# Attention and two feed-forward layers on one core: the first two blocks as one written list of single operations

## The chip, the cores and the metric

The kernel runs on one core of a Trainium2 chip. A core has TensorE (matmul, with its weight loads), VectorE, ScalarE, GpSimd and SyncE; in the profile they are PE (and PEld), DVE, ACT, POOL and SP. Each engine works through its own instructions in a fixed order and waits on semaphores for the others; data comes from and goes to device memory by DMAs, which SP, ACT and POOL issue. The metric is the device time of one execution in microseconds; of several executions the median counts.

## What is computed

Linear attention over 8 batches of 8 heads (576 positions, 64 wide) gives 4608 tokens of width 512. They go through a feed-forward layer with squared ReLU and then through one with SiLU, both 512 to 2048 to 512.

```python
def _attn_ref(q, k, v):
    q_s = np.exp(q - np.max(q, axis=-1, keepdims=True))
    q_s = q_s / (np.sum(q_s, axis=-1, keepdims=True) + 1e-09)
    k_s = np.exp(k - np.max(k, axis=2, keepdims=True))
    k_s = k_s / (np.sum(k_s, axis=2, keepdims=True) + 1e-09)
    kv = np.einsum('bhsd,bhse->bhde', k_s, v)
    return np.einsum('bhsd,bhde->bhse', q_s, kv)
def _moe_ref(x, w_in, w_out):        # then _moe2_ref, with h * sigmoid(h)
    r = np.maximum(x @ w_in, 0.0)
    return (r * r) @ w_out
# x = attention, tokens as rows: (4608, 512); out = _moe2_ref(_moe_ref(x))
```

The arrays are float32. For the layers the weights arrive as 64-bit words, of which the kernel makes a rounded float32 itself.

## The kernel before

The tokens are cut into 9 blocks of 512 (`NB`): block `i` below 8 holds the first 512 positions of batch `i`, block 8 the last 64 of every batch. A block has four pairs of heads (`pr` 0 to 3). For each pair the steps are: load keys, queries and values (`kv_load`, `q_load`, `v_load`; the remaining 64 positions of a batch come with `r_load`); the keys' maximum over positions (`kv_max`: three VectorE operations, then a transpose, a reduction, a scaled identity and a matmul that spreads it, `kv_tr`, `kv_red`, `kv_diag`, `kv_bc`; three pairs of block 0 use a GpSimd reduction over partitions instead); `kv_sub`, `kv_exp`, the product with the values `kv_mm`, the reciprocal `kv_rc` and the scaling `kv_scale`. Queries go through `q_max`, `q_sub`, `q_exp`, `q_norm`, `q_tr`, `q_hi`. Then `x_mm` gives the attention's output in PSUM, and `x_hi` (ScalarE) and `x_lo` (VectorE) split it into a high and a low float32r part.

The first layer has 16 column groups, here called weights 0 to 15. Each is loaded raw (`w1_load`), rounded (`w1_bits`, one ScalarE operation on the low words; `w1_round`, three VectorE operations: `TENSOR_SCALAR`, `SCALAR_TENSOR_TENSOR` and the custom integer addition) and split into a high part (`w1_hi`, ScalarE) and a low part (`w1_lo`, VectorE). For a block, a weight and a pair, `layer_part` issues three layer matmuls (high by high, high by low, low by high) into a bank `h`; four pairs make a group. `hidden` applies ReLU and square on ScalarE, `g_first` and `g_second` form sums for the next layer's Strassen-like products, `g_store` writes them to memory.

Every engine's instructions stay in the order in which the program writes them (`InOrder`, L73). For block 0, and for the attention of block 1, this order is a list of step names, `PLAN`; block 1's layer and all further blocks go through a loop over `n = i * 16 + t`, with steps hung into slots by the table `side` (`at`, `ORDER`, `SOONER`). After block 8 come three stages of Strassen-like products for the other three weight matrices; they take the time from about 500 us to the end.

SBUF is handed out as 73 rooms of one [128, 512] float32 each (`NU`; `room`, `back`, first in, first out). Raw weights of the first layer lie in three double rooms of `g_pool` and, early on, in the third of the `g_tiles`; rounded ones take a room (`wu`). The loop also rounds the second weight matrix to memory from block 3 on, through the same three double rooms. When block 8 starts, the rooms of the attention are given back, and the weights of the next stage are begun as rooms come free (`todo`, `begin`). The memory of `g_pool` becomes 9 further rooms after block 8.

Of the kernel before, what the change touches and what calls it, by code (L numbers as in the profile page):

```python
# [2 lines left out]

# [22 lines left out]
def kernel(  # L26
# [56 lines left out]
    P = 128  # L83
# [21 lines left out]
    PE_TR = (0, 1)  # L105

# [7 lines left out]
    NU = 73  # L114
# [3 lines left out]
    doubles, views = deque((-1, -2, -3, 0, 1, 2)), [0] * 3  # L118
    g_pool_was = tc.tile_pool(name="gpool", bufs=1)
    g_pool = g_pool_was.__enter__()  # L120

    def room(dt=F32, name="u"):
        n = rooms.popleft()
# [10 lines left out]
    def back(*ts):  # L134
        for t in ts:
            _, n, whence = lent.pop(id(t))
            whence.append(n)
# [28 lines left out]
    def raw_load(ph, f):  # L166

        if ph < 2:
            n = doubles.popleft()
            if n < 0:  # L170
                t = g_tiles[2].rearrange("p s c -> p (s c)").bitcast(I32)[:, 2 * TB * ~n:2 * TB * -n]
                lent[id(t)] = (t, n, doubles if views else [])
                views[:1] = []
            else:
                t = g_pool.tile([P, 2 * TB], I32, tag=f"d{n}", name="wraw")
                lent[id(t)] = (t, n, doubles)
            if ph:
                src = w_out[ph].bitcast(I32)[f * P:(f + 1) * P, :]
            else:
                src = w_in[ph].bitcast(I32)[:, 2 * f * P:2 * (f + 1) * P].rearrange(  # L180
                    "(c p) f -> p c f", p=P
                )
            sp.dma_start(out=t if ph else t.rearrange("p (c f) -> p c f", c=KC), in_=src)
            return [t]
# [50 lines left out]
    wh1, wl1, raw1 = {}, {}, {}  # L235

    def w1_load(x):
        raw1[x] = raw_load(*x)

    def w1_bits(x):  # L240
        to = []
        raw1[x] = to, rounding(0, raw1[x], to)
        next(raw1[x][1])

    def w1_round(x):
        to, going = raw1[x]
        for _ in going:
            pass
        raw1[x] = to[0]

    def w1_hi(x):
        wh1[x] = room(F32R, "wh")
        ac.copy(wh1[x], raw1[x])

    def w1_lo(x):
        u = raw1.pop(x)
        wl1[x] = room(F32R, "wl")
        ve.tensor_tensor(wl1[x], u, f32(wh1[x]), op=ALU.subtract)
        back(u)
# [112 lines left out]
    def kvf_store(b, pr):  # L372
        if pr == KC - 1:
            sp.dma_start(out=kvfd[b], in_=kvf_rooms[b % 2])
# [14 lines left out]
    kt, krt, vt, vrt, mt, mbt, held = {}, {}, {}, {}, {}, {}, {}  # L389

    def r_load(b, pr, dma=sp, dma2=sp):
# [3 lines left out]
        held[b] = [room(F32, "kr"), room(F32, "vr")]  # L395
        kr, vr = held[b][0], held[b][1][:, 0:KC * (D + 1)]
# [19 lines left out]
    def kv_load(b, pr, dma=sp):  # L416
# [15 lines left out]
        if b > 0 and pr == 0:  # L432
            r_load(b, pr)
# [27 lines left out]
    def kv_max(b, pr):  # L461
# [8 lines left out]
    mkt, kvps = {}, {}  # L470

    VIA_POOL = ((0, 1), (0, 2), (0, 3))
# [25 lines left out]
    def kv_sub(b, pr):  # L498
# [4 lines left out]
        )  # L503
        ve.tensor_tensor(tr, tr, mb, op=ALU.subtract)

    def kv_exp(b, pr):
        t, tr = kt[b, pr], krt[b, pr]
        ac.activation(t, t, AF.Exp)
        ac.activation(tr, tr, AF.Exp)


    def kv_mm(b, pr):
# [10 lines left out]
        if pr == KC - 1:  # L523
            back(*held.pop(b))
# [3 lines left out]
    def kv_rc(b, pr):  # L528
        rc = rct[b, pr] = spool.tile([P, 1], F32, tag="rc", name="rc", bufs=3)
        ve.tensor_scalar(rc, kvps[b, pr][:, 2 * P + D:2 * P + D + 1], EPS, None, op0=ALU.add)  # L530
        ve.reciprocal(rc, rc)
# [76 lines left out]
    def q_norm(i, pr):  # L608
# [3 lines left out]
        else:  # L612
            sm = spool.tile([P, 2, R, 1], F32, tag="sm", name="sm", bufs=6)
            ve.tensor_reduce(sm, t, axis=AX.X, op=ALU.add)
        ve.tensor_scalar(sm, sm, EPS, None, op0=ALU.add)
        ve.reciprocal(sm, sm)
        if i in PE_TR:
# [101 lines left out]
    def layer_part(t, c):  # L719
        if c == 0:  # L720
            first_h[t] = bank("h")
        h, f, (xh, xl) = first_h[t], FS[t], xs1[0, c]
# [4 lines left out]
        if t == NF - 1:  # L727
            back(*xs1.pop((0, c)))
# [3 lines left out]
    g_tiles.append(g_pool.tile([P, 7, TB], F32, tag="gs", name="gs"))  # L732

# [12 lines left out]
    def hidden(i, f, h):  # L746
# [6 lines left out]
        )  # L753
        ac.activation(o, o, AF.Square)
        back(h)

    def g_first(i, j):
        t = g_place(i, j)
        ve.tensor_tensor(t[:, S1], t[:, A21], t[:, A22], op=ALU.add)
        ve.tensor_tensor(t[:, S3], t[:, A11], t[:, A21], op=ALU.subtract)  # L760
# [17 lines left out]

    side = {}

    def at(i, slot, fn, *a):
        i, slot = divmod(max(0, i * NF + slot), NF)
        side.setdefault((i, slot), []).append((fn, a))
# [24 lines left out]
    at(1, 0, kvf_store, 1, KC - 1)  # L808
# [5 lines left out]
    for fn, d in ORDER:  # L814
        for nxt in range(2, NB):
            for pr, s in enumerate(BEGIN.get(nxt, (-12, -8, -4, 0))):
                if fn not in OF_KV or nxt < B:
                    if (fn, nxt, pr) in ((kv_load, 2, 0), (kv_load, 2, 1), (q_load, 2, 0)):
                        continue
# [285 lines left out]
    def store(u, half, ends):  # L1105
# [33 lines left out]
    wlist = [(0, f) for f in FS]  # L1139
    w2list = [(1, f) for f in range(NF)]  # L1140
    code_w = dict(w=w1_load, wbits=w1_bits, wround=w1_round, whi=w1_hi, wlo=w1_lo)
    code = dict(
        k=kv_load, q=q_load, v=v_load, kmax=kv_max, kred=kv_red, ksub=kv_sub, kexp=kv_exp,
        qmax=q_max, qsub=q_sub, qexp=q_exp, qnorm=q_norm, qtr=q_tr, qhi=q_hi, kvmm=kv_mm,
        ktr=kv_tr, kdiag=kv_diag, kbc=kv_bc, rc=kv_rc, scale=kv_scale, xmm=x_mm, xhi=x_hi, xlo=x_lo,
    )
    PLAN = """
        q00 k01 v00 q01 kmax00 w0 ktr00 qmax00 v01 kred00 qexp00 kmax01 q02 k02 w1 qmax01 kred01 v02 kdiag00
        qnorm00 qexp01 kbc00 ksub01 q03 qtr00 k03 ksub00 v03 qmax02 kexp00 qnorm01 w2 wbits0 kvmm00 qhi00
        kmax02 kexp01 wround0 kred02 k10 qtr01 qexp02 q10 kvmm01 rc00 w3 ksub02 v10 qmax03 qhi01 rc01 qsub03  # L1150
        k11 scale00 qnorm02 q11 whi0 xmm00 w4 kexp02 kmax03 v11 wbits1 wlo0 kred03 wbits2 qtr02 wround1 k12
        xhi00 kvmm02 q12 qexp03 qhi02 w5 xlo00 whi1 v12 wround2 h0.0 scale01 k13 xmm01 ksub03 whi2 q13 w6
        wlo1 kexp03 w7 rc02 qnorm03 h1.0 wbits3 w8 xhi01 kvmm03 scale02 xlo01 qtr03 xmm02 wlo2 qhi03 rc03
        wround3 h2.0 scale03 xhi02 h0.1 wbits4 xmm03 xlo02 w9 whi3 wround4 h1.1 xhi03 h1.2 h2.1 wlo3 w10 whi4
        xlo03 h0.2 wlo4 h0.3 kmax10 wbits5 h2.2 g0 kmax12 h1.3 wround5 ktr10 ktr12 g1 h3.0 h2.3 store0 kred10
# [213 lines left out]
```

## Time and profile before

| | |
|---|---|
| median of 3 runs | 1559.77 us (1559.12 to 1561.3) |
| the profiled execution | 1557.84 us |
| its span, first to last instruction | 1556.1 us |
| TensorE busy | 1525.5 us (98%) |
| VectorE, ScalarE, GpSimd busy | 1132.4 (73%), 899.9 (58%), 583.2 us (37%) |

The profile is of one execution. Busy time of a TensorE that is full says little of its pace, since matmuls overlap; idle time and the granted clock say what it lost. The span's parts have different limits, so the rows further down are by stretch.

### The profile page before, as it was taken

The numbers are of one execution on the slowest core, as the hardware profiler recorded it, in microseconds if no ns is written. First come the engines' busy times: TensorE is split into PE (matmuls) and PEld (weight loads), VectorE is DVE, ScalarE is ACT, GpSimd is POOL, SyncE is SP. The second block draws the span as 40 slices with busy tenths as digits, with TensorE's granted clock in tenths as the row PEclk, the third lists the DMA queues.
The fourth block names the chain that finished last, engine by engine and source line by source line (L and its number), as shares of the span: only waits on it lengthen the run. The fifth ranks groups of instructions, "written<-read, shape, count | busy, mean of one in ns | idle before, by whom it ended". The sixth has DMA issues, their size and how long they took to land.

```text
span 1556.1 us, 24775 instructions
## 1 busy us (share of the span) xinstructions
PE 1525.5 (98%) x7535; PEld 1301.5 (84%) x7535; DVE 1132.4 (73%) x2249; ACT 899.9 (58%) x1889; POOL 583.2 (37%) x892
## 2 busy tenths in 40 slices
PE   5899999999999999999999999999999999999997
PEld 4677888888888999999988988998888788888886
DVE  8978878986648877867798776766676964747344
ACT  6876766666546855555575664655556744554242
POOL 1135546655657020202144544444477040304120
PEclk8999999999999999999999999999999999999999
DMA  9659999998998898989897676867789776877562
GB/s 277 209 180 292 301 312 322 322 342 292 326 299 282 291 312 273 332 279 330 283 330 229 248 282 235 318 243 282 278 297 340 256 233 205 241 203 220 151 231 55
DMA packets 266919, 417.46 MB, mean 268 GB/s; under 512 B 69504, under 2 KB 188032, under 8 KB 266784
## 3 DMA queue, kind: packets, MB, share of 16 engines
q1 hardware_dynamic: 215664, 244.79, 51.7%
q0 software_dynamic: 48000, 169.65, 29.5%
q10 hardware_dynamic: 3120, 1.44, 0.4%
q8 instruction: 59, 0.97, 0.3%
q14 instruction: 76, 0.62, 0.1%
HBM read 234.62 MB, written 181.14 MB: 267 GB/s over the span
## 4 chain that ended last, share of the span: by engine, by line
PE 89%; DVE 5%; ACT 2%; DMA 1%; issue 1%; SPq 0%; POOL 0%; DVEq 0%; ACTq 0%; POOLq 0%
PE x L73 35%; PE h L73 21%; PE d L73 18%; PE a L73 9%; PE p L73 3%; PE kvps L73 2%; PE xps L73 1%; DVE wu L73 1%; ACT gs L73 1%; DVE xr L73 1%; DMA xr<-qd 0%; SPq L73 0%; DVE st L73 0%; DMA wraw<-in_moe_w_in_dram 0%; ACT q L73 0%
## 5 line engine op out<-in xcount | busy, mean ns | idle before, releaser
L73 DVE TENSOR_TENSOR al<-al,ah 128x460 fp32r<-128x460 f32 (+2 forms) x590 | 364.8, 658 | 187.3 <-ACT ah L73 177.8
L73 ACT CAST ah<-al 128x460 fp32r<-128x460 f32 (+2 forms) x590 | 326.7, 595 | 182.6 <-DVE al L73 39.5
L73 PE MATMUL h<-x,wh 128*128 128x512 f32 x1152 | 363.7, 397 | 1.1 <-DVE x L73 1.1
L73 PE MATMUL x<-ah,wT 128*128 128x460 f32 (+2 forms) x896 | 273.0, 375 | 0.0
L73 PEld LDWEIGHTS h<-x,wh 128*128 128x128 f32 x1152 | 213.6, 189 | 47.4 <-issue 2.9
L73 PE MATMUL h<-x,wl 128*128 128x512 f32 x576 | 225.3, 391 | 0.0
L73 ACT COPY st<-x 128x460 f32<-128x460 f32 (+2 forms) x175 | 95.8, 549 | 213.0 <-PE x L73 198.9
L73 POOL DMA_DIRECT2D g2d<-st x262 | 140.9, 543 | 129.9 <-ACT st L73 70.8
L73 PEld LDWEIGHTS x<-ah,wT 128*128 128x128 f32 x896 | 168.2, 188 | 23.7 <-ACT st L73 0.8
L73 PE MATMUL x<-al,wT 128*128 128x460 f32 (+2 forms) x448 | 168.0, 375 | 0.0
L73 ACT ACTIVATE gs<-h 128x512 f32<-128x512 f32 x144 | 85.9, 596 | 128.5 <-PE h L73 126.0
L73 POOL TENSOR_TENSOR gs<-gs 128x256 f32<-128x256 f32 x128 | 110.6, 866 | 108.4 <-DVE gs L73 62.9
L73 POOL DMA_DIRECT2D out_dram<-st x128 | 68.2, 541 | 209.7 <-DVE st L73 203.5
L73 PE MATMUL a<-ah,wB 128*128 128x460 f32 (+2 forms) x448 | 141.0, 375 | 0.0
L73 PE MATMUL d<-ah,wT 128*128 128x460 f32 (+2 forms) x448 | 136.5, 375 | 0.0
L73 PE MATMUL x<-ah,wB 128*128 128x460 f32 (+2 forms) x448 | 136.4, 375 | 0.0
L73 PE MATMUL x<-ah,wN 128*128 128x460 f32 (+2 forms) x448 | 136.4, 375 | 0.0
L73 PE MATMUL d<-ah,wB 128*128 128x460 f32 (+2 forms) x448 | 136.3, 375 | 0.0
L73 PEld LDWEIGHTS h<-x,wl 128*128 128x128 f32 x576 | 108.4, 188 | 23.5 <-DVE wl L73 0.2
L73 DVE TENSOR_TENSOR st<-st 128x460 f32<-128x460 f32 (+1 forms) x161 | 101.2, 654 | 25.9 <-ACT st L73 21.8
L73 DVE TENSOR_TENSOR gs<-gs 128x256 f32<-128x256 f32 x160 | 83.7, 530 | 31.4 <-ACT gs L73 18.3
L73 POOL DMA_DIRECT2D g1d<-gs x80 | 70.8, 886 | 79.8 <-ACT gs L73 62.8
(135 smaller groups left out, 2737.9 us busy)
## 6 DMA issues: line engine op xcount, KB each, us to landing
al<-g2d SPq DMA_DIRECT2D x240, 256.0 KB, 3.3
g1d<-gs POOLq DMA_DIRECT2D x64, 896.0 KB, 7.1
al<-g1d SPq DMA_DIRECT2D x224, 230.0 KB, 4.3
g2d<-st POOLq DMA_DIRECT2D x210, 230.0 KB, 4.1
al<-g1d SPq DMA_DIRECT2D x56, 232.0 KB, 4.1
al<-x2d SPq DMA_DIRECT2D x56, 230.0 KB, 5.3
x2d<-st POOLq DMA_DIRECT2D x53, 230.0 KB, 5.8
g2d<-st POOLq DMA_DIRECT2D x52, 232.0 KB, 3.6
```

Of the source, the lines that this page charges most:

```text
L73: got = fn(*a, **kw)
```

## The change

1. `PLAN` now holds blocks 0 and 1 whole, with block 1's layer (`h1.t.c`), and much of the attention of blocks 2 and 3. The loop starts at `n = 2 * NF`. What the list holds is taken out of the loop's slots (`planned`).
2. Seven helpers yield after each operation (`PIECES`: maximum, subtraction and exponential of the keys, their reciprocal, the queries' normalising, `hidden`, `g_first`), as does `w1_round`. A name in the list advances its helper by one operation, so that other steps can stand between. `q_out` and `r_load` have names of their own.
3. Raw weights of the first layer have fixed places (`raw_homes`, in the second and third `g_tiles` and in a pool of its own), and are rounded in place: the second and third operation write the low and the high words of the raw array, 8 bytes apart, and `w1_hi` and `w1_lo` read the high words there. The first operation writes `w_bits`.
4. In block 0 pair 3 follows pair 0, then pairs 1 and 2; single loads of block 1 stand among block 0's.
5. After block 0's third reduction GpSimd adds two [128, 1] tiles; the ones of the value tiles are set at the start.
6. There are 71 rooms. The pool of raw weights and value tiles is closed when block 8 starts and gives 11 rooms there; the remaining 7 come after block 8.

```diff
+    NU = 71 - 4 * len(PAIRS)          # PAIRS is empty
 def room(dt=F32, name="u"):
-        t = (upool if n < NU else rpool[0]).tile([P, TB], dt, tag=f"u{n}", name=name)
+        t = (upool if n < NU else rpool[n < NU + 7]).tile([P, TB], dt, tag=f"u{n}", name=name)
...
+    def w1_bits(g):
+        low, _ = raw1[g]
+        ac.activation(low, low.bitcast(U32), AF.Copy, scale=2.0 ** -29)
+    def w1_round(g):
+        low, high = raw1[g]
+        o = w_bits[:, 0:len(WGROUPS[g]) * TB]
+        ve.tensor_scalar(o, high, 0x07FFFFFF, 3, op0=ALU.bitwise_and, op1=ALU.logical_shift_left)
+        yield
+        ve.scalar_tensor_tensor(low, high, -0x40000000, low, op0=ALU.bitwise_and, op1=ALU.bitwise_or)
+        yield
+        ve.tensor_tensor(high, o, low, op=ALU.add)
...
     def kv_max(b, pr):
         ve.tensor_tensor(m1, t[:, :, 0:2, :], t[:, :, 2:4, :], op=ALU.max)
+        yield
         ve.tensor_tensor(m2, m1[:, :, 0, :], m1[:, :, 1, :], op=ALU.max)
+        yield
         ve.tensor_tensor(m2, m2, tr, op=ALU.max)
...
         if (b, pr) in VIA_POOL:
             gp.partition_all_reduce(mbt[b, pr], m, P, bass_isa.ReduceOp.max)
+            via_pool.append(pr)
+            if len(via_pool) == len(VIA_POOL):
+                gp.tensor_tensor(warm[1], warm[0], warm[0], op=ALU.add)
...
+    PLAN = """
+        k0.3 q0.3 q0.0 w0 kmax0.0 kmax0.0 v0.0 k0.1 kmax0.0 w1 ktr0.0 kmax0.3 v0.3 kred0.0 kmax0.3 kdiag0.0 qmax0.3
...
+    for what in PLAN:
+        fn, a = arguments(what)
+        if fn in PIECES or fn is w1_round:
+            if (fn, a[:2]) not in going:
+                going[fn, a[:2]] = fn(*a)
+            next(going[fn, a[:2]], None)
+        else:
             fn(*a)
...
-    for n in range(NF, NB * NF + 6):
+    for n in range(2 * NF, NB * NF + 6):
...
         if n == (NB - 1) * NF:
+            raw_pool_was.__exit__(None, None, None)
+            rpool.append(ctx.enter_context(tc.tile_pool(name="rpool", bufs=1)))
+            rooms.extend(range(NU + 7, NU + 18))
```

How the rows of an engine move is seen at three places. VectorE, in the middle of block 0: before, with the maximum of pair 2's keys (`xr`, `m`), the rounding of weight 0 (`wu`), a reciprocal (`rc`) and the subtraction for the same keys:

```order
L73 TENSOR_TENSOR xr_305<-k_237 128x256
L73 TENSOR_TENSOR m_238<-xr_305 128x128
L73 TENSOR_TENSOR m_238<-m_238,kr_167 128x128
L73 TENSOR_SCALAR wu_292<-gs_156 128x512
L73 SCALAR_TENSOR_TENSOR wu_292<-gs_156,wu_292 128x512
L73 ISA wu_292<-gs_156,wu_292 128x1024
L73 TENSOR_SCALAR rc_356<-kvps_214 128x1
L73 RECIPROCAL rc_356<-rc_356 128x1
L73 TENSOR_TENSOR k_237<-k_237,m_238 128x512
```

And a stretch of the changed order, with the roundings of weights 5 and 6 (`wu1` is `w_bits`, `gs_159` and `wraw_160` the raw arrays) and block 1's subtractions:

```order
L74 TENSOR_SCALAR wu1_161<-gs_159 128x512
L74 TENSOR_TENSOR k_377<-k_377,kvps_585 128x512
L74 SCALAR_TENSOR_TENSOR gs_159<-gs_159 128x512
L74 TENSOR_REDUCE mx_629<-q_469 128x8
L74 ISA gs_159<-gs_159,wu1_161 128x512x2
L74 TENSOR_TENSOR q_469<-q_469,mx_629 128x512
L74 TENSOR_TENSOR kr_304<-kr_304,kvps_585 128x128
L74 TENSOR_SCALAR wu1_161<-wraw_160 128x512
L74 TENSOR_TENSOR q_452<-q_452,mx_601 128x512
```

Steps of one rounding stood next to each other; now another operation stands between any two.

ScalarE, late in block 0: before, with the bit steps of the last two weights (`wraw`), the copy of an attention output (`x`), the exponential of block 1's keys (`k`, `kr`) and a high part (`wh`):

```order
L73 ACTIVATE wraw_880<-wraw_880 128x512
L73 ACTIVATE wraw_896<-wraw_896 128x512
L73 CAST x_942<-xps_917 128x512
L73 ACTIVATE k_374<-k_374 128x512
L73 ACTIVATE kr_320<-kr_320 128x128
L73 CAST wh_957<-wu_889 128x512
```

The changed order where the exponentials of the last two of block 1's key pairs stand (`k_428`, `k_480`; `wraw_160` holds weight 13):

```order
L74 ACTIVATE wraw_160<-wraw_160 128x512
L74 CAST wh_889<-gs_159 128x512
L74 CAST x_897<-xps_874 128x512
L74 ACTIVATE k_428<-k_428 128x512
L74 ACTIVATE kvf_375<-kvps_724,rc_876 64x64 x2
L74 ACTIVATE k_480<-k_480 128x512
```

The bit steps of weights 14 and 15 come some 15 and 20 rows behind these now.

SP, the first loads: before, with the remaining keys `kr`, queries, keys, values and the first raw weight (`gs_156`):

```order
L73 DMA kr_167<-in_k_dram 64x4x64 x2
L73 DMA q_196<-in_q_dram 128x2x256
L73 DMA k_198<-in_k_dram 128x2x256
L73 DMA v_162<-in_v_dram 128x4x64
L73 DMA v_163<-in_v_dram 128x4x64
L73 DMA q_207<-in_q_dram 128x2x256
L73 DMA gs_156<-in_moe_w_in_dram 128x4x256
L73 DMA v_200<-in_v_dram 128x4x64
L73 DMA v_201<-in_v_dram 128x4x64
L73 DMA q_235<-in_q_dram 128x2x256
```

Changed, with pair 3's keys and queries (`k_208`, `q_215`), pair 0's queries (`q_217`) and the first two weights (`gs_158`, `gs_159`):

```order
L74 DMA kr_173<-in_k_dram 64x4x64 x2
L74 DMA k_208<-in_k_dram 128x2x256
L74 DMA q_215<-in_q_dram 128x2x256
L74 DMA q_217<-in_q_dram 128x2x256
L74 DMA gs_158<-in_moe_w_in_dram 128x4x256
L74 DMA v_168<-in_v_dram 128x4x64
L74 DMA v_169<-in_v_dram 128x4x64
L74 DMA k_225<-in_k_dram 128x2x256
L74 DMA gs_159<-in_moe_w_in_dram 128x4x256
L74 DMA v_210<-in_v_dram 128x4x64
```

Pair 0's queries moved from the second to the fourth place, and a weight moved ahead of the values.

## Rows read from the trace of the kernel before

**Rows 1.** Busy time by stretch (us, instructions), granted clock, DMA share and rate.

```profile
core 0: us, PE busy (x) PEld busy (x) DVE busy (x) ACT busy (x) POOL busy (x), PEclk, DMA share, GB/s
0.00:31.00 31.00, 15.38 (x103) 10.03 (x105) 25.92 (x84) 21.71 (x78) 5.09 (x16) 0.85 1.06 266
25.00:30.00 5.00, 4.12 (x7) 2.15 (x7) 4.86 (x12) 3.47 (x8) 0.00 (x0) 0.50 1.18 302
31.00:80.00 49.00, 43.94 (x243) 32.65 (x240) 45.15 (x97) 39.10 (x94) 5.00 (x8) 0.99 0.75 230
80.00:160.00 80.00, 78.67 (x466) 61.81 (x465) 66.11 (x157) 56.21 (x123) 37.29 (x46) 1.00 0.76 236
160.00:1540.00 1380.00, 1379.77 (x6701) 1191.16 (x6700) 992.47 (x1911) 781.71 (x1595) 535.86 (x823) 1.00 0.82 273
447.00:480.00 33.00, 33.00 (x150) 27.46 (x150) 13.94 (x21) 17.45 (x33) 23.02 (x31) 1.00 0.75 239
```

**Rows 2.** Waits of TensorE, 0 to 120 us: in total, times, longest.

```profile
PE kvps L73 <- ACT k L73: 3.8, 2, 2.6
```

**Rows 3.** The chain that ended last, 60 to 92 us: start, us, what.

```profile
70.01 5.93 DMA wraw<-in_moe_w_in_dram
...
75.96 0.65 ACT wraw L73
...
77.09 0.53 ACT k L73
...
85.16 2.76 PE h L73 x12
```

**Rows 4.** Timeline of VectorE, 37 to 43 us: start, us, operation.

```profile
37.88 0.68 DVE L73 TENSOR_TENSOR wl<-wu,wh 128x512 fp32r<-128x512 f32 x1
38.48 0.42 DVE L73 TENSOR_TENSOR xr<-k 128x256 f32<-128x256 f32 x1
38.93 0.29 DVE L73 TENSOR_TENSOR xr<-xr 128x128 f32<-128x128 f32 x1
39.26 0.29 DVE L73 TENSOR_TENSOR xr<-xr,kr 128x128 f32<-128x128 f32 x1
39.47 0.42 DVE L73 TENSOR_TENSOR xr<-k 128x256 f32<-128x256 f32 x1
...
40.46 0.42 DVE L73 TENSOR_SCALAR wu<-wraw 128x512 int32<-128x512 int32 x1
40.91 0.69 DVE L73 SCALAR_TENSOR_TENSOR wu<-wraw,wu 128x512 int32<-128x512 int32 x1
41.74 0.69 DVE L73 CUSTOM_DVE_ANT_0 wu<-wraw,wu 128x1024 uint16<-128x1024 uint16 x1
```

**Rows 5.** Timeline of TensorE, 86 to 95 us.

```profile
91.04 0.69 PE L73 MATMUL kvps<-v,k 128*64 128x65 f32 x16
...
91.77 2.38 PE L73 MATMUL xps<-xr,kvf 128*128 128x512 f32 x4
93.58 1.03 PE L73 MATMUL h<-x,wh 128*128 128x512 f32 x2
```

**Rows 6.** Timeline, 93 to 104 us; in brackets the idle time before and its releaser.

```profile
97.44 0.68 DVE L73 TENSOR_REDUCE mx<-q 128x8 f32<-128x512 f32 x1
...
102.45 2.04 POOL L73 TENSOR_TENSOR q<-q,mx 128x512 f32<-128x512 f32 x2 [8.15 <-DVE gs L73]
...
103.52 0.64 ACT L73 ACTIVATE q<-q 128x512 f32<-128x512 f32 x1 [2.46 <-POOL q L73]
```

**Rows 7.** Groups by form on ScalarE, 4 to 80 us: busy, mean ns | idle before, releaser.

```profile
L73 ACT CAST wh<-wu 128x512 fp32r<-128x512 f32 x14 | 8.6, 615 | 6.8 <-DVE wu L73 6.8
...
L73 ACT ACTIVATE wraw<-wraw 128x512 int32<-128x512 uint32 x10 | 6.7, 667 | 3.0 <-DMA wraw<-in_moe_w_in_dram 3.0
```

**Rows 8.** Waits of VectorE, 0 to 130 us: in total, times, longest.

```profile
DVE m L73 <- DMA kr<-in_k_dram: 1.3, 1, 1.3
DVE mx L73 <- DMA q<-in_q_dram: 1.2, 2, 0.8
```

More of the change, by code (lines that the diff above doesn't have):

```diff
@@ L2 @@
 from contextlib import ExitStack
+from itertools import count
 import concourse.bass as bass
@@ L105 @@
     PE_TR = (0, 1)
+    FIRST = 4
+    WGROUPS = [(x,) for x in range(16)]
+    PAIRS = [x for x in WGROUPS if len(x) > 1]
     spool = ctx.enter_context(tc.tile_pool(name="spool", bufs=1))
@@ L233, in rounding @@
         to.append(u)
[L235 to L259, printed above, removed]
+    wh1, wl1, raw1, wr1, w_pairs = {}, {}, {}, {}, {}
@@ L261, in round_to_dram, with w1_back @@
+    def w1_back(*ts):
+        for t in ts:
+            if w_pairs[id(t)]:
+                lent[id(t)] = (t, id(t), r_rooms)
+            back(t)
     def round_to_dram(ph, f):
@@ L436, with v_ones @@
     v_tiles = {}
+    def v_ones():
+        for n in range(3):
+            v_tiles[n] = raw_pool.tile([P, 2, R, D + 1], F32, name=f"v{n}")
+            gp.memset(v_tiles[n][:, :, :, D:D + 1], 1.0)
     def v_rooms(b, pr):
@@ L522, in kv_mm @@
         back(*held.pop((b, pr)))
-        if pr == KC - 1:
+        left[b] -= 1
+        if not left[b]:
             back(*held.pop(b))
@@ new lines, with arguments @@
+    """.split()
+    def arguments(what):
+        name = what.rstrip("0123456789.-")
+        return CODE[name], tuple(None if x == "-" else int(x) for x in what[len(name):].split("."))
+    planned = {arguments(what) for what in PLAN if not what[0] == "h"}
+    planned = {(fn, a) for fn, a in planned if fn not in (r_load, hidden, kvf_store) and fn.__name__[:3] != "w1_"}
+    planned = {(fn, a) for fn, a in planned if a[0] is None or fn is g_again or a[0] > (fn not in (g_first, g_second, g_store))}
@@ L1196 @@
     ve.memset(kv_room[:, 0:P], 1.0)
+    going = {}
     for what in PLAN:
-        run(what)
-    kvf_store(0, KC - 1)
-    for n in range(NF):
-        for fn, a in side.pop((0, n), ()):
+        fn, a = arguments(what)
+        if fn is hidden:
+            fn, a = hidden, (a[0], FS[a[1]], first_h[a])
+        if fn in PIECES or fn is w1_round:
[3 more added lines that the diff above has]
+        else:
             fn(*a)
@@ L1280 @@
                 spare = 2 + AHEAD + SPLIT - held_by(1) - 2 * (NF - 1 - t)
-                while todo and len(doing) < 6 and len(rooms) - owed[0] >= todo[0][0] + max(0, spare):
+                while todo and len(doing) < 6 and len(rooms) + len(r_rooms) - owed[0] >= todo[0][0] + max(0, spare):
                     begin()
                 go_on()
-    assert not side
+    assert not side and not planned
     g_pool_was.__exit__(None, None, None)
-    rpool.append(ctx.enter_context(tc.tile_pool(name="rpool", bufs=1)))
-    rooms.extend(range(NU + 7, NU + 16))
+    rpool.append(ctx.enter_context(tc.tile_pool(name="rpool2", bufs=1, side="right")))
     banks.extend(a_banks)
```

247 lines of the change are left out of this document (161 added, 86 removed).

## Prediction

> **What bounds the kernel now.** I read the stretches first [rows 1]. From 160 to 1540 us TensorE is busy 1379.77 of 1380 us: nothing that the change does there can gain more than a quarter of a microsecond. The tail behind 1540 is not touched. What TensorE loses lies in front: it stands idle for 15.62 us of the first 31 and for 5.06 us of the next 49, and for 1.33 us between 80 and 160. [...] As it is full from there on, the kernel's time moves by what this arrears moves.
>
> Who makes it wait? VectorE is busy 25.92 + 45.15 = 71 of these 80 us, ScalarE 61 [rows 1]. TensorE's longest wait after the start is for an exponential on ScalarE, 2.6 us [rows 2]. The chain [rows 3] shows what is behind it: a raw weight takes 5.93 us to land, ScalarE waits for it in its fixed order, and the x copy and block 1's key exponential stand behind. That load could only be issued when VectorE had rounded an earlier weight. So VectorE's pace, and the fixed order on ScalarE, set the arrears.
>
> **Part by part. (1) Single operations on VectorE.** Rows 4 give two prices. A 512-wide operation whose input was not just written follows after 0.60 us (37.88 to 38.48, while the operation lasts 0.68: the next begins before the last has ended). One that reads what the operation before it wrote follows later: after the 256-wide maximum 0.45 us for an operation of 0.42, a 128-wide one 0.33 against 0.21 without such a dependence (38.93 to 39.26, 39.26 to 39.47), and inside a rounding 0.45 and 0.83 us (40.46, 40.91, 41.74). A dependent follower thus costs 0.12 to 0.23 us; I take 0.13. Up to the low part of the last weight, VectorE's written order before has 71 such pairs; the changed one has 15, since pieces of maximum, rounding, normalising and reciprocal now alternate. 56 pairs at 0.13 are 7.3 us of VectorE's time.
>
> Not all of it reaches TensorE, because other work was moved ahead. I count both orders with the same prices: 0.60 for a 512-wide operation, 0.35 for the first one of a rounding, 0.36 and 0.21 for the 256- and 128-wide, 0.1 for the tiny ones, 0.13 on top for a dependent one, from the first operation at 4.2 us. TensorE's work at full clock: 0.23 us a layer matmul (12 take 2.76 us [rows 3]), 0.73 for a pair's 20 products, 0.91 for an attention product [rows 5], and some 0.1 to 0.2 for a transpose. What counts is, for each weight, VectorE's work ahead of it less TensorE's work ahead of its first use: so much TensorE has lost by then at least. Weights are counted from 0.
>
> Before, the worst is weight 13: 76 operations of 512, 16 first ones, 8, 27 and 26 small ones and 69 pairs make 71.5 us, so it is there at 75.7 at the earliest; ahead of it TensorE has 158 layer matmuls (36.2) and 12.1 us of attention: 27.4 lost. [...] After, weight 13 needs only 66.2 us, and the worst place moves: weight 15 (88 of 512, 16, 9, 31 and 32 small ones, 15 pairs: 73.5, so 77.7; TensorE 176 layer matmuls, 40.3, and 14.5 of attention) gives 22.9, and the last input of block 1 (pair 2, VectorE 85.9, TensorE 62.7) 23.2. The arrears shrink from 27.4 to 23.2: **4.2 us**. The early waits of VectorE (1.3 us for block 0's remaining keys, 1.2 for queries [rows 8]) are left out of both.
>
> [...]
>
> **(2) The first loads.** Pair 3 now comes second, and query 0 is SP's third load behind the remaining keys, not the first. VectorE waited 1.2 us for queries before, in two pieces [rows 8]; query 0 now lands two issues later, and VectorE has pair 3's maximum and query meanwhile. Bounds: 2 us lost, if the queries of pair 1, now behind two weights, come late as well; 1 us won, since ScalarE makes the scaled identity for pair 0's key maximum ahead of the query's eight exponentials, and no longer between two such groups. I take 0. What is cover here is VectorE's backlog; without it each of these waits is paid in full.
>
> **(3) Late weights.** The last two raw weights still wait for VectorE to free their places, but block 1's key exponentials now stand ahead of their bit step on ScalarE. [...] The next in line is then VectorE, as counted.
>
> **(4) Raw weights in place.** The rounding now writes its second and third step with a gap of one element, and the high copy and the low part read with such a gap. ScalarE's gapped step takes 667 ns, a dense copy 615 [rows 7]: at most 0.05 us each, 16 times, 0.8 us on ScalarE. VectorE reads the gapped raw weight before too (0.69 to 0.83 between steps [rows 4]). A gapped write of VectorE is not in these rows. Its bounds are 0 and one more half-width operation's worth, 0.53 us (0.68 for 512 against 0.42 for 256 columns, twice the difference [rows 4]), for 32 writes. I take 0, the value of the reads.
>
> **(5) GpSimd's early addition.** Its first subtraction of block 2's queries starts at 102.45, although its maximum ran from 97.44: some 4.3 us late, and ScalarE waits 2.46 us for it [rows 6]. TensorE works through this; of its 1.33 us idle between 80 and 160 at most all could hang on the late block 2. Bounds 0 and -1.3; I take 0, for no row ties them. [...]
>
> **(6) Rooms for the last block.** Eleven rooms come 50 us sooner. TensorE is busy 33.00 of 33 us there, with VectorE at 14 [rows 1]: 0. The two rooms fewer in the blocks between (71 for 73) lie under the same full TensorE: 0, and their bound is the slack of a load issued twelve steps ahead.
>
> **Sum.** 1557.84 us for the profiled execution (span 1556.1 and 1.74 around it) less 4.2 is 1553.6. That execution was 1.93 below the shown median of 1559.77; the runs after should centre on 1559.77 - 4.2 = **1555.6 us**. About 0.2%, 3.1 us, is what a measurement can tell from no change.
>
> **Rivals.** *New waits take the gain.* ScalarE's own count is now close: up to weight 11's high part it has 56.8 us behind its start at 7.5, TensorE 42.6: 21.7. Before, ScalarE stood idle for 19 of the first 80 us, of these 6.8 for the roundings and 3.0 for raw weights [rows 7]. If 4 to 6 us of such waits remain, ScalarE ends last and the arrears are 26 to 28: 1558 to 1561. For it: in the new order every piece waits for another engine. Against: the pieces between give each answer time. *All goes well.* GpSimd's 1.3 goes too, and VectorE loses 2 us less at the start: 1552.2. *The written gap costs (the slower side).* At 0.13 us for each of 32 writes the 4.2 us are gone; at 0.53 VectorE has 17 us more ahead of weight 15, and the time is 1559.77 + 17 - 4.2 = 1572.6. For it: no such write in the rows; against: gapped reads are free. *Order does nothing.* If every pair costs alike, the 56 pairs cost 7.3 us as before and the work moved ahead remains: weight 15 at 30.2 against 27.4, 1562.6. [...] *The change doesn't do what it says:* the rooms given back are used by nobody in time; that is nil anyway.
>
> **Numbers.** Forecast 0.46 (1553 to 1557), all well 0.15, new waits 0.27, gap 0.07, order nothing or a worse start 0.05. Faster by over 0.2% needs 1556.6 or less: all well and most of the forecast, 0.58. Within 0.2%: new waits and the weak end of the forecast, 0.30. Slower: 0.12. The range 1551 to 1561.5 takes in the first three and leaves out the gap and some of both ends.
>
> **What would show it.** In the changed profile: TensorE's idle time up to 80 us near 16 to 17 us instead of 20.7; layer matmuls of weight 13 starting about 5 us sooner; operations of one rounding 0.6 us apart with another between; VectorE's gapped writes still at 0.69; GpSimd's first subtraction right behind its maximum. I am wrong if TensorE's wait moves to ScalarE's copies of the high parts, if gapped writes last 0.8 or more, or if TensorE has idle time between 160 and 1540.

## The result: 16.5 us slower, and where it shows

The changed kernel takes 1576.40 us (median of 4 runs, 1573.55 to 1578.89) against 1559.94 us for the kernel before in the same comparison: a ratio of 1.0104, 95% interval 1.0085 to 1.0123. The profiled execution took 1576.83 us, its span is 1575.1 us, 19.0 us longer than before. The forecast was 1555.6 us, with 1551 to 1561.5 us as the range. It was wrong in sign and by 21 us.

The stretches of the changed kernel, as [rows 1] were read before; the stretch from 160 on is split at block 8. TensorE's idle time is the length of a stretch less its busy time, and PEclk is the granted clock as a share of full speed. From 160 to 447 us TensorE is busy all 287 us.

```profile
core 0: us, PE busy (x) PEld busy (x) DVE busy (x) ACT busy (x) POOL busy (x), PEclk, DMA share, GB/s
0.00:31.00 31.00, 18.07 (x114) 11.76 (x114) 25.09 (x89) 22.56 (x80) 5.68 (x20) 1.00 0.97 252
31.00:80.00 49.00, 44.94 (x265) 34.10 (x264) 44.50 (x105) 40.90 (x105) 5.37 (x9) 1.00 0.81 232
80.00:160.00 80.00, 70.28 (x375) 53.91 (x374) 53.00 (x127) 46.28 (x94) 30.50 (x37) 0.96 0.72 228
...
447.00:510.00 63.00, 57.89 (x263) 48.05 (x262) 38.72 (x56) 30.83 (x60) 41.90 (x53) 0.95 0.76 252
510.00:1540.00 1030.00, 1029.08 (x4806) 901.68 (x4805) 718.39 (x1345) 565.00 (x1167) 334.69 (x577) 1.00 0.79 264
```

Up to 80 us TensorE is idle for 12.93 + 4.06 = 17.0 us, 3.7 us less than before [rows 1], as the forecast had it ("near 16 to 17 us"). Three more traces of the same program up to there (e1, e2 and e3 below) show 17.7 to 18.7, so against the one trace of before this gain is 2.0 to 3.7 us. By 100 us it is gone (in e1 to e3 the idle time is then above that of before); the first row is the kernel before, the second the changed one:

```profile
0.00:100.00 100.00, 79.11 (x443) 57.63 (x444) 83.77 (x210) 75.69 (x206) 13.09 (x30) 0.95 0.82 231
0.00:100.00 100.00, 79.11 (x456) 57.01 (x457) 87.09 (x236) 76.65 (x211) 18.14 (x37) 1.00 0.81 230
```

What took it stands between 82 and 94 us, where TensorE had no wait before. The first row is the first layer matmul of weight 13 in the kernel before, the second the same matmul in the changed kernel (start, duration, operation; in brackets the idle time and its releaser):

```profile
81.27 0.62 PE L73 MATMUL h<-x,wh 128*128 128x512 f32 x2
82.34 0.73 PE L74 MATMUL h<-x,wh 128*128 128x512 f32 x2 [1.79 <-ACT gs L74]
...
92.86 0.33 PE L74 MATMUL kvps<-ident,xr 128*128 128x128 f32 x1 [1.38 <-DVE xr L74]
```

The forecast's other sign, "layer matmuls of weight 13 starting about 5 us sooner", did not come: they start 1.1 us later, with some 3 us more of attention work ahead of them in TensorE's order (an estimate at the prediction's prices: one attention output, one product with the values, two queries' transposes and one spread maximum). They wait for a ReLU on ScalarE, ahead of which the bit step of raw weight 14 waits for its load:

```profile
81.13 0.67 ACT L74 ACTIVATE wraw<-wraw 128x512 int32<-128x512 uint32 x1 [1.93 <-DMA wraw<-in_moe_w_in_dram]
81.70 0.58 ACT L74 ACTIVATE gs<-h 128x512 f32<-128x512 f32 x1
```

Two holes come on top. From 80 to 160 us TensorE is idle for 9.72 us in all (1.33 before), 5.26 of them at 112 us, and for 5.11 us in block 8, where there was nothing. First the hole at 112 us, in the timelines of TensorE, SyncE and VectorE:

```profile
117.70 0.47 PE L74 MATMUL kvps<-ident,xr 128*128 128x128 f32 x1 [5.26 <-DVE xr L74]
...
118.25 1.20 PE L74 MATMUL h<-x,wh 128*128 128x512 f32 x2
...
123.56 0.71 PE L74 MATMUL h<-x,wh 128*128 128x512 f32 x2
```

```profile
101.25 1.08 SPq L74 DMA_DIRECT2D qd<-q  x2
...
107.47 1.75 SPq L74 DMA_DIRECT2D xr<-qd  x4
109.26 0.43 SPq L74 DMA_DIRECT2D q<-in_q_dram  x1
109.74 0.47 SPq L74 DMA_DIRECT2D k<-in_k_dram  x1
```

```profile
113.63 0.69 DVE L74 TENSOR_REDUCE mx<-q 128x8 f32<-128x512 f32 x1 [3.40 <-DMA q<-in_q_dram]
114.58 1.15 DVE L74 TENSOR_TENSOR xr<-k 128x256 f32<-128x256 f32 x1 [0.26 <-DMA k<-in_k_dram]
```

Read from the bottom. In the written list VectorE's next steps at 110 us are the maxima of block 3's first queries and keys (`qmax3.0`, `kmax3.0`). Their loads (`q3.0`, `k3.0`) went out only at 109.3 and 109.7, because SyncE's order has `qback2.1` ahead of them, and that waits for a store of transposed queries to land, that is, to have arrived in memory; SyncE issues nothing between 105.5 and 107.47. VectorE stands 3.7 us, and all its other work of block 2 stands behind. TensorE's transpose `ktr3.0` stands ahead of block 1's next layer matmuls in its order, so these wait too. Behind the hole the granted clock reads 0.65 from 115 to 120 us and 0.67 from 120 to 125, and two layer matmuls take 1.05 to 1.20 us, against 0.62 to 0.71 from 123.56 on: the nine layer matmuls and three attention products from 118.25 to 123.43 take 5.2 us, where 12 at 0.23 [rows 3] would take 2.8.

The hole in block 8, from the timelines of ScalarE, GpSimd and TensorE:

```profile
490.28 0.41 ACT L74 CAST wT<-wt 128x256 fp32r<-128x256 f32 x1 [10.45 <-POOL wt L74]
490.59 0.59 ACT L74 ACTIVATE gs<-h 128x512 f32<-128x512 f32 x1
```

```profile
477.34 12.23 POOL L74 TENSOR_TENSOR wt<-wB,wt 128x256 f32<-128x256 f32 x15
```

```profile
491.24 1.22 PE L74 MATMUL h<-x,wh 128*128 128x512 f32 x2 [5.11 <-ACT gs L74]
...
495.24 0.68 PE L74 MATMUL h<-x,wh 128*128 128x512 f32 x2
```

With the rooms given back, the preparation of product weights goes further inside block 8 than before. GpSimd gets 15 subtractions in a row, and a copy of one result (`wT`) stands in ScalarE's order ahead of the next ReLU. ScalarE waits 10.45 us for it; nobody empties TensorE's banks, and TensorE stops. The same row of GpSimd is in the kernel before:

```profile
466.04 12.13 POOL L73 TENSOR_TENSOR wt<-wB,wt 128x256 f32<-128x256 f32 x15
```

but there no `wT` copy had been begun by then, and ScalarE's waits in this stretch were for TensorE. The nine layer matmuls behind the hole take 4.0 us, 1.9 more than 9 x 0.23.

**The sum.** The first matmul of the second stage (`x<-ah,wB`, at the end of block 8) starts at 499.32 us before and at 515.07 after: 15.75 us later. From the rows: 3.7 less idle up to 80; 9.72 - 1.33 = 8.4 more from 80 to 160 (3.9 of the 9.72 ahead of 100), and 2.4 by the clock behind the hole; 5.1 + 1.9 in block 8: 14.1 of 15.75. Behind that point the changed kernel loses another 3.2 us with TensorE full but for one wait of 0.6; no run shows a cause for the rest. Together that is the 19.0 us between the two profiled executions; the medians lie 16.5 apart.

### The profile page after: what moved, and what is told of

It reads as the page before. It is cut to its first block, busy times and chain, and to the rows that moved or that the text cites. A ratio compares the mean times of both kernels' runs of the same rounds, so it can differ in the third digit from the quotient of the medians.

```text
span 1575.1 us, 24761 instructions
## 1 busy us (share of the span) xinstructions
PE 1533.5 (97%) x7535; PEld 1305.8 (83%) x7535; DVE 1127.4 (72%) x2249; ACT 898.6 (57%) x1889; POOL 583.6 (37%) x893
## 4 chain that ended last, share of the span: by engine, by line
PE 86%; DMA 4%; DVE 4%; SPq 2%; ACT 2%; issue 2%; POOL 1%; DVEq 0%; POOLq 0%; ACTq 0%
PE x L74 34%; PE h L74 20%; PE d L74 17%; PE a L74 9%; PE p L74 3%; SPq L74 2%; PE kvps L74 2%; PE xps L74 1%; DMA wraw<-in_moe_w_in_dram 1%; DMA k<-in_k_dram 1%; DMA al<-x2d 1%; DVE xr L74 1%; ACT gs L74 0%; DVE st L74 0%; DMA wB<-wd 0%
```

## Experiments

The last column is that first matmul of the second stage in each run's trace; it contains all that the change does, without what follows. The runs come from several comparisons, in which the kernel before took 1558.1 to 1560.3 us; between comparisons go by the ratios.

| run | made from | median us | ratio to before (95%) | second stage starts |
|---|---|---|---|---|
| kernel before | | 1559.8 | 1 | 499.32 |
| changed kernel | | 1576.4 | 1.0104 (1.0085 to 1.0123) | 515.07 |
| e1 rooms late | changed | 1569.6 | 1.0061 (1.0046 to 1.0076) | 509.94 |
| e2 loads early | changed | 1574.2 | 1.0089 (1.0071 to 1.0106) | 514.76 |
| e3 both | changed | 1563.7 | 1.0025 (1.0015 to 1.0034) | 504.20 |
| e4 whole helpers | e3 | 1573.1 | 1.0084 (1.0069 to 1.0099) | 514.45 |
| e5 no addition | e3 | 1565.6 | 1.0042 (1.0029 to 1.0055) | 504.49 |
| e6 bit steps later | e3 | 1565.1 | 1.0034 (1.0022 to 1.0046) | 503.18 |
| e7 transposes later | e6 | 1563.4 | 1.0029 (1.0018 to 1.0040) | 502.59 |
| e8 other places | e3 | 1562.9 | 1.0027 (1.0017 to 1.0037) | 502.61 |
| e9 e8, with e6's load and e7's transposes | e8 | 1561.8 | 1.0015 (1.0005 to 1.0025) | 500.70 |
| e10 products later | e9 | 1563.1 | 1.0020 (1.0008 to 1.0031) | 503.47 |
| e11 more products later | e10 | 1565.8 | 1.0035 (1.0023 to 1.0047) | 509.12 |
| e12 three begun | e9 | 1561.9 | 1.0010 (0.9999 to 1.0021) | 500.53 |
| e13 values first | e12 | 1562.1 | 1.0011 (1.0002 to 1.0020) | 500.53 |

One caution on the traces. Kernels that are the same up to some point don't run the same up to it: e9 and e10 have one program up to 96 us, and TensorE is busy 63.8 and 60.1 us of the first 80. A single trace of the start is good to some 2 us either way; the medians decide.

**e1: the rooms.** They are handed out behind the loop, no longer at the start of block 8.

```diff
             rpool.append(ctx.enter_context(tc.tile_pool(name="rpool", bufs=1)))
-            rooms.extend(range(NU + 7, NU + 18))
...
     rpool.append(ctx.enter_context(tc.tile_pool(name="rpool2", bufs=1, side="right")))
+    rooms.extend(range(NU + 7, NU + 18))
```

> The changed kernel, but the 11 rooms are handed out only after the loop over the blocks, as the 9 were before. Theory A (the rooms let product weights begin in block 8 whose copies to a high part on ScalarE stand ahead of ReLUs and wait 10.45 us for GpSimd's burst of 15 subtractions): TensorE's wait of 5.1 us at 486 and the stretch of 0.50 clock behind it go, 7.5 us in all, and the time is about 1576.4 - 7.5 = 1569 us. Theory B (the wait at 486 comes of the block's own late start, or of GpSimd's burst, which was there before too): a wait of 3 us or more stays between 447 and 520, and the time is 1574 to 1577 us.

1569.6 us, as theory A said. Block 8 is full again, at full clock:

```profile
447.00:510.00 63.00, 63.00 (x296) 52.76 (x295) 36.15 (x56) 34.24 (x62) 44.35 (x55) 1.00 0.78 256
```

**e2: the loads.**

```diff
-klo2.0 r3
+klo2.0 q3.0 k3.0 r3
...
-h1.4.0 q3.0 h1.4.1 sumb1.0 k3.0 h1.4.2 qback2.0
+h1.4.0 h1.4.1 sumb1.0 h1.4.2 qback2.0
```

> The changed kernel, but the loads of block 3's first queries and keys (q3.0, k3.0) are issued ahead of block 2's remaining positions and of the transposed queries, which wait on SyncE 1.9 us for a store to land. Theory A (VectorE stood in its order at these two loads, 3.4 + 0.3 us, and TensorE's transpose of block 3's maximum stood behind): TensorE's wait of 5.3 us at 112 and the two stretches at 0.65 and 0.67 behind it go, some 8 us, and the time is about 1568 us. Theory B (VectorE's work behind the loads, or the remaining positions that now land later, is what is late): the wait moves a few microseconds on, the gain is under 3 us, 1573 us or more.

1574.2 us: a gain of 2.2, not 8. The wait of 5.26 is gone; TensorE's waits for `xr` from 100 to 160 us are now

```profile
PE kvps L74 <- DVE xr L74: 3.0, 2, 1.8
```

so in part it moved, as theory B has it. The intervals of e2 and the changed kernel overlap; that the edit gains is clear only from e1 to e3.

**e3: both.**

> Both edits together. If the two waits are all that makes the changed kernel slow and they add up: 1576.4 - 7.5 - 8 = 1561 us or a little less, within 2 us of the kernel before, with TensorE's idle time up to 80 us still 17 us. If one of the two only moves: 1566 to 1570. If the early gain of 2.7 us at 80 us comes through whole, 1558.

1563.7 us, 12.7 below the changed kernel, and the second stage starts 10.9 us sooner. That lies between the two forecasts, 1561 if both waits are all and 1566 if one only moves. The edit of the loads is worth 2.2 us on the changed kernel and 5.9 on e1, that of the rooms 6.8 and 10.5; with intervals of some 3 us on the changed kernel and e2 this does not show that one needs the other. But 4 us more than before remain. TensorE's waits from 80 to 160 us in e3:

```profile
PE kvps L74 <- DVE xr L74: 3.9, 4, 1.7
PE h L74 <- ACT gs L74: 2.1, 1, 2.1
```

**e4: whole helpers, the price of a dependent pair.** The pieces of `kv_max`, `kv_rc`, `q_norm` and `w1_round` run together at the place of the last one (`n` is the place in the list, `final` the last place of a name):

```diff
+        if fn in (kv_max, kv_rc, q_norm, w1_round):
+            if final[what] == n:
+                for _ in fn(*a):
+                    pass
+            continue
```

> Both edits, and the key maximum, the reciprocal of the keys, the queries' normalising and the rounding are written whole again, at the place of their last piece, so that dependent operations stand side by side as they did before. Theory A (a dependent follower costs VectorE 0.12 to 0.23 us more, 56 pairs up to the last weight of the first layer's block 0): VectorE is some 7 us later at 75 us, of which 4 us reach TensorE, and the time is 4 us above that of the kernel with both edits. Theory B (every pair costs alike): within 1.5 us of it, but for what the shifted first pieces do.

Theory A, by more than its size: 9.4 us above e3. VectorE's timeline in e3, with the pieces apart:

```profile
36.51 0.42 DVE L74 TENSOR_TENSOR xr<-k 128x256 f32<-128x256 f32 x1
36.84 0.42 DVE L74 TENSOR_SCALAR wu<-gs 128x512 int32<-128x512 int32 x1
37.17 0.28 DVE L74 TENSOR_TENSOR xr<-xr 128x128 f32<-128x128 f32 x1
37.38 0.68 DVE L74 SCALAR_TENSOR_TENSOR gs<-gs 128x512 int32<-128x512 int32 x1
37.98 0.28 DVE L74 TENSOR_TENSOR xr<-xr,kr 128x128 f32<-128x128 f32 x1
```

and in e4, a rounding and a maximum whole:

```profile
51.13 0.42 DVE L74 TENSOR_SCALAR wu<-wraw 128x512 int32<-128x512 int32 x1
51.46 0.69 DVE L74 SCALAR_TENSOR_TENSOR wraw<-wraw 128x512 int32<-128x512 int32 x1
52.19 0.69 DVE L74 CUSTOM_DVE_ANT_0 wraw<-wraw,wu 128x1024 uint16<-128x1024 uint16 x1
52.80 0.42 DVE L74 TENSOR_TENSOR xr<-k 128x256 f32<-128x256 f32 x1
53.25 0.29 DVE L74 TENSOR_TENSOR xr<-xr 128x128 f32<-128x128 f32 x1
53.57 0.29 DVE L74 TENSOR_TENSOR xr<-xr,kr 128x128 f32<-128x128 f32 x1
```

What follows the 256-wide maximum comes after 0.33 us if it does not read it and after 0.45 if it does; for the 128-wide one 0.21 and 0.32; for the rounding's second step 0.60 and 0.73. The price is 0.11 to 0.13 us for a pair. How much of the 9.4 us this makes is not shown. By the names in the traces some 50 pairs come back, not 56: rounded in place, the second step no longer reads the first, and follows it after 0.33 us (0.45 before [rows 4]). That is an estimated 6 us of VectorE's time; besides, the whole helpers start their first pieces later, which this run does not hold apart.

**e5: without GpSimd's addition.**

```diff
-            if len(via_pool) == len(VIA_POOL):
-                gp.tensor_tensor(warm[1], warm[0], warm[0], op=ALU.add)
```

> Both edits (rooms late, loads of block 3 early), without GpSimd's early addition. Theory A (the wait of some 4 to 7 us that stands before GpSimd's first arithmetic operation only moves from about 18 us, where GpSimd has nothing to do, to the first subtraction of block 2's queries at 80.68, and the exponentials behind it hold ScalarE up, which holds TensorE's banks): GpSimd's first subtraction starts 4 us or more behind the maximum's end, TensorE loses 2 to 5 us more between 80 and 100 us, and the time is 1566 to 1569 against 1563.7 us with the addition. Theory B (the subtraction is not tied, as the prediction took it): within 1 us of 1563.7.

GpSimd's first subtraction now starts 7.8 us behind the end of the maximum that it needs; in e3 it is 0.1 us (80.54 and 80.68). In the changed kernel (first two rows) the wait stands ahead of the addition, where no engine is seen to wait for it; without it (last two rows) it stands ahead of the subtraction:

```profile
25.11 0.28 POOL L74 TENSOR_TENSOR warm<-warm 128x1 f32<-128x1 f32 x1 [7.27 <-issue]
79.66 1.04 POOL L74 TENSOR_TENSOR q<-q,mx 128x512 f32<-128x512 f32 x1 [3.89 <-DVE mx L74]
```

```profile
78.29 0.68 DVE L74 TENSOR_REDUCE mx<-q 128x8 f32<-128x512 f32 x1
86.78 1.03 POOL L74 TENSOR_TENSOR q<-q,mx 128x512 f32<-128x512 f32 x1 [11.60 <-DMA q<-in_q_dram]
```

The profile puts this wait down to the load of the queries, but they had landed when the maximum was taken from them. That the wait moves is shown. What it costs is not settled: by the ratios 0.0017, some 2.7 us, but the intervals of e3 and e5 overlap, and the second stage starts only 0.3 us later.

**e6, e7: users later.** e6 puts `wbits14` and `wbits15` behind the second piece of `g0.11` and `k3.2` ahead of `qback2.0`; e7 also moves `ktr2.2`, `ktr2.1`, `ktr3.0` and `ktr3.2` a few matmuls back.

> Both edits, and two more moves of loads against their users: ScalarE's bit steps of weights 14 and 15 come after the hidden part of weight 11, no longer ahead of those of 10 and 11, and the load k3.2 is issued in front of a transposed query's four loads instead of behind eight. If waits for a landing that stand in an engine's order ahead of other work are the cause: TensorE's wait of 2.1 us at 81.6 (h behind ACT gs) goes to under 0.5, and that of 1.7 at 126 (kvps behind DVE xr) to under 0.8; with the half clock behind them 3 to 5 us, 1559 to 1561. If VectorE is what is late: they become waits for DVE wl or xr of the same length, 1563 to 1564.

> As the run with later bit steps, and four transposes of key maxima (two of block 2, two of block 3) stand some matmuls later in TensorE's order, which fills the time in which VectorE makes their input. If TensorE's remaining waits between 80 and 160 us are for these four (1.0, 0.3, 0.9 and 1.7 us with both edits): they fall to under 1 us together and the time is 1 to 3 us below that run, 1557 to 1559, below the kernel before (1559.8). If VectorE's chain behind the transposes is the limit, they come back at the next product: no difference.

e6 gained nothing (its interval overlaps that of e3). e7 came out 1.7 us below e6, as hoped, but their intervals overlap too, and it stays above the kernel before; its waits for `xr` fell from 2.4 to 1.6 us, those for `kvx` stayed (1.5 and 1.7). In e6 the wait for `gs` is gone, and one for the weight itself stands in its place, 3 us on:

```profile
85.09 0.73 PE L74 MATMUL h<-x,wh 128*128 128x512 f32 x2 [1.37 <-ACT wh L74]
```

So weight 14 is late, and not only in front of others. The chain that ended last in e3 says why: its raw load takes 6.77 us and goes out only at 75.69, behind VectorE's work on earlier weights in the same places.

```profile
74.93 0.60 DVE wl L74
...
75.69 6.77 DMA wraw<-in_moe_w_in_dram
...
82.49 0.67 ACT wraw L74
```

**e8, e9: other places for weights 14 and 15.**

```diff
-(raw_pair, 1), (raw_one, 0), (raw_pair, 0), (raw_pair, 1),
+(raw_pair, 1), (raw_one, 0), (raw1_, 0), (raw2_, 0),
...
-qmax1.1 w13
+qmax1.1 w13 w14
...
-wlo10 scale1.3
+wlo10 w15 scale1.3
...
-kvmm1.2 w14 store0.4 wround13 w15 xmm1.1
+kvmm1.2 store0.4 wround13 xmm1.1
```

> Both edits (rooms late, loads of block 3 early), and raw weights 14 and 15 get places that are free long before (the two of weights 2 and 10, in slots of the second and third g tile that block 0 does not write), so that their loads no longer wait for the low parts of weights 11 and 12. Theory A (the chain low part, load of 6.8 us, bit step, rounding, copy is what is late at weight 14): the raw weight lands before 76 us, TensorE's wait of 2.1 us at 81.6 and the two for DVE xr at 93 and 94 (1.3 us) go, no clock under 1.00 at 85 to 90, and the time is 3 to 5 us below that of both edits (ratio to the kernel before 1.0025): 0.9995 to 1.0005. Theory B (VectorE's or ScalarE's own work up to weight 14 is late): waits for wh, wl or xr of 2 us or more stay between 80 and 95, ratio 1.002 to 1.003.

> As the run with the two other places, and the load k3.2 earlier and four transposes of key maxima later in TensorE's order. If the waits that are left (for kvps at 114 and 128) are for these: 1 to 2 us below that run, ratio 0.998 to 0.9995. If VectorE's work behind them is the limit: the same as that run within 1 us.

In e8's chain no raw weight is left between 60 and 95 us, and the waits for `gs` and `wh` behind weight 14 fell to one of 0.38 us for a low part; the second stage starts 1.6 us sooner than in e3. The ratio (1.0027) did not move beyond its interval, as theory B has it, though the waits went as theory A says: those for `xr` at 112 and 126 us grew instead, from 0.94 and 1.68 us in e3 to 1.30 and 1.96. With e6's load of `k3.2` and e7's transposes (e9) the ratio is 1.0015, which overlaps e8's, and the second stage starts 3.5 us sooner than in e3. TensorE's waits from 80 to 160 us in e9:

```profile
PE kvps L74 <- ACT kvx L74: 2.1, 2, 1.3
PE kvps L74 <- DVE xr L74: 1.0, 2, 0.7
PE xps L74 <- ACT kvs L74: 0.6, 2, 0.4
PE h L74 <- DVE wl L74: 0.4, 1, 0.4
```

**e10: products later in TensorE's order.** 14 attention products of blocks 2 and 3 stand one to three groups of layer matmuls later.

> As the run with the two other places and the four later transposes; besides, from block 1's layer on, 14 attention products of TensorE (maxima spread, products with the values, attention outputs of blocks 2 and 3) stand one to three groups of layer matmuls later in TensorE's order, none behind the first step that uses it. Nothing moves on another engine. Theory A (TensorE's fixed order puts products in front of layer matmuls whose inputs are there long since; the waits of 1.3, 0.75, 0.4 and 0.2 us between 112 and 131 are for order alone): these waits fall to under 1 us together, the half-clock stretches with them, and the ratio to the kernel before is 0.9985 to 1.0005. Theory B (the engines behind a product need it at once, so that a product issued later makes the next one later): the same waits come back at other products, ratio 1.001 to 1.002.

Theory B: the waits moved to the next products (0.82, 0.63 and 1.48 us) and the ratio is 1.0020. A further run (e11) with 30 products moved, from block 0 on, came out at 1.0035 (1.0023 to 1.0047); in it a product of block 1 (`kvmm1.1`) stands behind the load that overwrites its values (`v2.0`), so that this part computes from other values, and only its time is used. Moving TensorE's share of these chains later makes what hangs on them late: the second stage starts at 503.47 us in e10 and 509.12 in e11, against 500.70 in e9.

**e12: the rooms early, fewer begun.**

```diff
-                while todo and len(doing) < 6 and len(rooms) + len(r_rooms) - owed[0] >= todo[0][0] + max(0, spare):
+                while todo and len(doing) < 3 and len(rooms) + len(r_rooms) - owed[0] >= todo[0][0] + max(0, spare):
```

> As the run with the two other places and later transposes (ratio 1.0015), but the 11 rooms come at the start of block 8 again, as in the changed kernel, while at most three weight preparations (not six) may be under way in that block. Theory A (it is not the rooms that cost, but how many preparations they let stand in ScalarE's fixed order ahead of ReLUs at one time): GpSimd's longest row of subtractions falls from 15 to about 6, ScalarE waits under 3 us for it at a time, TensorE does not wait between 447 and 510, and the ratio is that of the run it is made from, 1.000 to 1.002. Theory B (any copy that waits for GpSimd holds up the ReLUs): TensorE waits 2 to 5 us in block 8 and the ratio is 1.003 to 1.006. In neither case do the early rooms gain time, since TensorE had no wait there before.

Theory A. GpSimd's longest row is 6 subtractions (4.57 us), TensorE has no wait in block 8. ScalarE's longest wait for `wt` in that stretch, 10.45 us in the changed kernel, is now

```profile
ACT gs L74 <- POOL wt L74: 1.1, 1, 1.1
```

With three begun at a time the early rooms cost nothing that shows, and they gain nothing either: 1.0010 against 1.0015, intervals that overlap.

**e13: block 0's values first.** `v1.2`, `r1` and `w3` go behind the loads of block 0's values on SyncE; no other engine's order changes.

> As the run with at most three preparations (ratio 1.0010), and SyncE loads the values of block 0's pairs 1 and 2 ahead of block 1's first values, of block 1's remaining positions and of weight 3; no other engine's order changes. Theory A (the written order puts loads of block 1 ahead of block 0's values, so that TensorE's two products with them at 20.5 and 24.4 wait 0.75 + 0.56 us and its work stays thin until 28 us, in which two layer matmuls last 1.22 us instead of 0.62): these waits go, the layer matmuls last 0.62 from 26 us on or sooner, and the ratio is 0.9990 to 1.0003. Theory B (VectorE's and ScalarE's first inputs, or VectorE's count of operations, set the first 35 us): the waits become waits for DVE x or for weights, ratio 1.0005 to 1.002.

Theory B. The waits for values at 20 and 24 us went and waits for `xr` (1.7 us at 22) and `x` (1.65 at 32) came, as long or longer; the second stage starts at 500.53 as in e12. By these waits the start is set by VectorE and ScalarE, not by the loads of the values.

No run beats the kernel before; e12 cannot be told from it.

## Why the prediction was wrong

**The frame was the error.** It said that TensorE is full from 160 us on, so that the time moves by its arrears at that point, and then it counted the arrears up to weight 15 and block 1's last input. Inside the count term (3), below, failed: by 100 us TensorE has the same 20.9 us of idle time as before. Two more places lay outside the count.

- *80 to 160 us.* The list also holds some 200 steps of blocks 2 and 3. They had no term of their own but "new waits", which looked for them on ScalarE's copies of high parts. The wait was one queue further: SyncE, whose order puts a load behind a wait for a landing, and VectorE behind that load. The row said 1.33 us idle from 80 to 160 [rows 1]; the prediction took it to hold for the new order too. Shown by the trace and by e2 and e3 (2.2 to 5.9 us).
- *Term (6), rooms for the last block, priced at 0* since TensorE is "busy 33.00 of 33 us there". It cost 7 us (trace), 6.8 by e1 and 10.5 by e2 and e3. The cover named was TensorE's own work, which says what a late room would cost, not what an early one sets off. The step left out is who gets work because of the rooms, and what that work stands ahead of on an engine with a fixed order. e12 shows that it was this, and not the rooms.

**Term (1), dependent pairs: right, and the size of one pair right.** 0.13 us was taken; e3 and e4 show 0.11 to 0.13. The 27.4 and 23.2 us that its 4.2 comes from are the author's estimates from prices in the rows, and no run shows them; the traces show TensorE's idle time up to 80 us, 20.7 us before [rows 1] and 17.0 in the changed kernel. Of the 4.2 us, 2.0 to 3.7 show as idle time less up to 80 us, and e4 loses 9.4 us, in part because pairs come back. But the gain does not reach the end: with both holes removed (e3) 4 us more than before remain, with weight 14 and the transposes moved 2.3 (e9).

**Term (2), first loads: 0 did not hold on VectorE.** Up to 35 us it waits 2.5 us for loads before, 3.8 us in the changed kernel and 4.7 to 5.7 in e1, e2, e3 and e12: the waits for queries went, and one of 1.8 to 3.2 us for raw weight 2 came, near 28 us. What that is worth at the end is not shown; in e13 this wait is gone, and nothing was gained.

**Term (3), late weights: failed.** "The next in line is then VectorE, as counted" left the load itself out: a place freed by VectorE, 6.5 to 6.8 us of landing and the bit step still end the chain at weight 14. ReLUs now stand behind the bit step in place of the exponentials, and TensorE waits 1.79 us for one of them at 82 us. With an earlier load (e8) the second stage starts 1.6 us sooner. **Term (4), gapped writes: 0 held.** The next operation follows a gapped write after 0.60 us (37.38 to 37.98 in e3). **Term (5): the late start is there without the addition, and the addition hides it.** In the changed kernel 7.27 us of idle time stand ahead of the addition; without it (e5) 7.8 us lie between the maximum and the subtraction, with it (e3) 0.1. The wait is shown, its cause by no run. Its worth in this order, 0.3 us by the start of the second stage and 2.7 by the ratios, may be more than the 1.3 allowed.

**Two readings** are off without moving the sum. "0.69 to 0.83 between steps": 0.69 is how long the steps last, and between them [rows 4] show 0.45 and 0.83. And the row of the first 31 us gives a clock of 0.85 on average [rows 1], while the durations there are longer than that alone would make them: 16 products of keys and values last 1.14 us at 14, 16, 23 and 30 us and 0.69 at 91 [rows 5].

**The rivals.** "New waits take the gain" was the right kind with the wrong place and at most a quarter of the size; its price was bounded by waits of the kernel before, and a new order makes waits that it did not have. None of the rivals on the slower side was what happened. The list of what would prove the forecast wrong did name it: "if TensorE has idle time between 160 and 1540".

**What stays open:** the 3.2 us that the changed kernel loses behind 515 us (1.1 to 1.8 in the variants with late or few preparations; the first 1200 matmuls of the second stage take 249.2 us in the changed kernel, e1, e3, e9 and e12 alike and 248.0 before, without a wait), and the last 1.2 us or so by which e9, e12 and e13 are later than before at the second stage, although TensorE is busy 63.8 us of the first 80 in e9 and 59.3 before [rows 1]. The waits left in e9 are, but for 0.4 us, in the attention of blocks 2 and 3; e10 shows that they are not TensorE's order alone.

## What to carry over

In a written order for several engines, go through each queue for places where an instruction that waits for a landing stands ahead of one that does not: a load behind such a wait is late for everything in its user's queue (here VectorE stood 3.7 us and TensorE 5.26), and the holes add up (both edits of e3 together gained 12.7 us, alone 6.8 and 2.2). Memory that comes free sooner is not neutral where a planner turns it into work: look up on which in-order engine that work then stands, and ahead of what (here on ScalarE ahead of a ReLU, a wait of 10.45 us). A stretch in which the bottleneck is full tells what a delay costs there, not that nothing can empty it.

## What the hardware showed that was not expected

- The two holes of 5 us cost some two fifths as much again by the clock: behind those at 112 and 486 us the next 12 and 9 matmuls of the layer and the attention take 5.2 and 4.0 us, which is 2.4 and 1.9 us more than at 0.23 each [rows 3]. The granted clock reads 0.65 on average from 115 to 120 us and, behind the second hole,

```profile
490.00:495.00 5.00, 3.76 (x9) 3.00 (x10) 4.67 (x4) 2.94 (x6) 4.92 (x8) 0.50 0.57 198
```

- Near the start of the changed kernel the clock column shows no lower level: it says 1.00 from 24 to 28 us, yet two layer matmuls last 1.22 us there and 0.63 from 33 us on. Durations of like matmuls are the better witness there.

```profile
24.00:28.00 4.00, 3.95 (x28) 3.24 (x28) 2.10 (x7) 3.01 (x9) 1.41 (x5) 1.00 1.04 324
```

```profile
25.58 1.22 PE L74 MATMUL h<-x,wh 128*128 128x512 f32 x2
...
33.19 0.63 PE L74 MATMUL h<-x,wh 128*128 128x512 f32 x2
```
